# ConvNeXt-V2 block: the order of SyncE's DMA issues within a slot

## Chip, cores and metric

The kernel runs on one core of a Trainium2 chip. The metric is the device time of one execution in microseconds (us). SyncE (SP) computes nothing here; it issues DMAs from one list, in the order of the program, and where an issue has to wait, all that stands behind it waits too.

## What is computed

One block on an image of 512 x 512 pixels with 96 channels, in bf16: a depthwise 3x3 convolution, a layer norm over the channels, a product with w1 (96 to 384), GELU, a global response norm over all pixels, a product with w2 (384 to 96), and the residual.

```
out = sum over i, j of xp[:, i:i+H, j:j+W, :] * dw[i, j]
h = layernorm(out)
h = gelu(h @ w1)
gx = sqrt((h * h).sum(axis=(1, 2)) + 1e-6)
nx = gx / (gx.mean(axis=-1) + 1e-6)
h = grn_gamma * (h * nx) + grn_beta + h
return x + h @ w2
```

The response norm needs the sum of squares of h over the whole image, so the kernel makes two passes.

## The kernel before

The image is cut into 128 blocks of 4 rows. The **first pass** makes conv, layer norm, the w1 product, GELU and the sums of squares. The **second pass** (lines 1017 to 1040) makes or reloads h for each block, multiplies by w2 and adds x. The change lies in the first pass alone.

The first pass is a software pipeline over slots (the loop at line 838), one block per slot in the steady part. A block goes through these stages, each in a later slot than the one before. Each engine's instructions are kept in program order (the class InOrder, so most lines of the profile read L35, its helper).

- `load_x(s + 4)`: SP loads block s + 4 into `xin` (4 buffers). `turn_x(s + 3)`: DVE transposes block s + 3 into `xT`; a block loaded in slot s is thus turned in slot s + 1, in the middle of DVE's work there.
- `conv_taps(s)`: PE makes the convolution, and ACT, in some slots helped by DVE, copies it out of PSUM to `y_bf` (`evac`).
- `stage_sq`: POOL squares `y_bf` (`ysq`). `stage_stats`: PE sums y and y squared over the channels. `stage_moments`: DVE scales the sums.
- For each batch of four blocks: `stage_rstd` and `stage_newton`, twelve small POOL operations that make the reciprocal standard deviation (`var`, `ri`, `nt`, `rn`, `rstd`); `stage_turn`, a DVE transpose to `rt` in the same slot as the Newton steps; one slot later `stage_rows`, two SP DMAs that write `rt` to `r_dram`; one slot later `stage_bcast`, four SP DMAs that read it back to all partitions as `rbc` (3 buffers).
- `stage_norm`: POOL multiplies `y_bf` by `rbc` to `yn` (3 buffers). The first norm of a batch comes one slot after the broadcast.
- One slot later `stage_write`, four SP DMAs of `yn` to `yn_dram`; one slot later `stage_read`, one SP DMA back to `ynT` in the layout that PE needs; two slots later the w1 product of that block (`mlp_units`), GELU on ACT into `g`, `bn_stats` on DVE (`bst`) for the sums of squares, and Gram products on PE for the rest.
- `store_next`: SP writes a third of a finished `g` to `g_dram`, for blocks whose h is kept for the second pass.

The table built at lines 798 to 832 says in which slot each stage of each block or batch falls. Rows and broadcast of one batch thus never fall into the same slot; of four slots one has rows and the next one the broadcast. Within a slot the order of SP's issues is the order of the calls at lines 840 to 850. POOL's order in a slot is newton, square, norm, rstd. The first four blocks and the last fourteen go other ways: the first make their rstd on DVE and PE, without rows and broadcast, and after the conv of block 127 the slots have the w1 product alone (`mlp_tail`).

Of the kernel before, what the change touches and what calls it, by code (L numbers as in the profile page):

```python
# [56 lines left out]
def kernel(  # L57
# [129 lines left out]
    with ExitStack() as p1:  # L187
# [31 lines left out]
        def load_x(b):  # L219
            t = xinpool.tile([128, SL, C], bf16, name="xin")  # L220
            off = x.offset + b * GR * W * C
            rows = lambda p0, p1, s0, s1: (
                t[p0:p1, s0:s1, :].rearrange("p g c -> p (g c)"),
                bass.AP(x.tensor, off + (p0 * PXP - 1 + s0) * C, [[PXP * C, p1 - p0], [1, (s1 - s0) * C]]))
            if b == 0:
                pool.memset(t[0:1, 0, :], 0.0)
                parts = [(16, 128, 0, SL), (0, 16, 1, SL), (1, 16, 0, 1)]
            elif b == NBLK - 1:
                pool.memset(t[96:128, SL - 1, :], 0.0)
                parts = [(0, 112, 0, SL), (112, 128, 0, SL - 1), (112, 127, SL - 1, SL)]  # L230
            else:
                parts = [(0, 128, 0, SL)]
            for part in parts:
                o, i_ = rows(*part)
                sp.dma_start(out=o, in_=i_)
            xins[b] = t
# [377 lines left out]
        def stage_rows(k):  # L614
            b0, n = BATCHES[k]
            rt = rts.pop(k)
            N = n * GR * NG
            nq, nt = min(32, N), (N + 31) // 32
            with nc.allow_non_contiguous_dma("small rows of rstd"):
                if nq == 32:  # L620
                    for t in range(nt):
                        sp.dma_start(
                            out=r_dram[b0:b0 + n].rearrange("b r w -> (b r w)").rearrange(
                                "(t q a p) -> t a q p", q=32, a=4, p=32)[t],
                            in_=rt[:, 32 * t:32 * t + 32])
                else:
                    for a in range(4):
                        sp.dma_start(
                            out=r_dram[b0:b0 + n].rearrange("b r (g m) -> (b r g) m", g=NG)[:, 32 * a:32 * a + 32],
                            in_=rt[32 * a:32 * a + nq, :32])  # L630

        def stage_bcast(k):
            b0, n = BATCHES[k]
            rbc = rbcpool.tile([128, BATCH, W], bf16, name="rbc")
            for j in range(GR):
                sp.dma_start(out=rbc[32 * j:32 * j + 32, :n, :].rearrange("p n w -> p (n w)"),
                             in_=bass.AP(r_dram[b0].tensor, r_dram[b0].offset + j * n * W, [[0, 32], [1, n * W]]))
            rbcs[k] = rbc
# [9 lines left out]
        def stage_write(b):  # L648
            yn = yns.pop(b)
            for r in range(GR):  # L650
                sp.dma_start(out=yn_dst(b, r), in_=yn[32 * r:32 * r + 32, :, :])
# [101 lines left out]
        def store_next():  # L753
            if stores:
                b, h = stores.pop(0)
                n = NCH * QW * NQ // 3
                sp.dma_start(out=g_dram[whole.index(b)][:, h * n:h * n + n],
                             in_=flat(b)[:, h * n:h * n + n])
# [78 lines left out]
        turn_x(2)  # L837
        for s in range(last_slot + 1):
            get = lambda kind: at.get((s, kind), [])
            if s + 4 < NBLK:  # L840
                load_x(s + 4)
            for b in get("read"):
                stage_read(b)
            for b in get("write"):
                stage_write(b)
            for k in get("bcast"):
                stage_bcast(k)
            for k in get("rows"):
                stage_rows(k)
            store_next()  # L850
            for k in get("newton"):
                stage_newton(k, pool)
# [218 lines left out]
```

## Time and profile before

| | |
|---|---|
| median of the 3 runs | 1477.81 us (1477.04 to 1479.55) |
| span of the profiled execution, first to last instruction (no other time is listed for it) | 1475.6 us |
| busy share of the span: PE, DVE, ACT, POOL | 94%, 80%, 95%, 88% |
| DMA issues of SP in the change: rows, broadcasts | 62 of 8 KB, 124 of 128 KB |
| other DMA issues of SP in the first pass: x loads, yn writes, yn reads, g stores | 132, 512, 128, 105 |
| length of one norm, one square on POOL | 3.11 us, 2.76 us |

The span can be read in stretches: to about 70 us the start, to 870 the steady first pass, to 973 its end without convolutions, and then the second pass. A wait in the profile is the idle time of an engine ahead of an instruction, with the name of what released it; for a wait on a DMA the name is that of an issue near the release, and it can be that of a neighbour in SP's queue. SP's own lines give the time in which it issued, not the time of the transfer.

### The profile page before, as it was taken

What the parts mean: (1) busy time and instruction counts of PE and PEld (TensorE: products, weight loads), DVE (VectorE), ACT (ScalarE), POOL (GpSimd) and SP (SyncE); (2) the same over time, 40 slices, a digit from 0 to 9 for tenths busy, and PEclk for the clock granted to TensorE, in tenths of its full rate; (3) what the DMA queues carried; (4) which work ended last, traced back from release to release, by engine and by line L of the source; (5) the groups of instructions that cost most, each with busy time, mean ns of one, the idle gap of its engine ahead of it and who ended that gap; (6) DMA issues with size and microseconds to landing.
All of it is one profiled execution on the core that took longest, in us unless ns stands there. A gap on an engine that the chain in (4) does not pass through costs nothing.

```text
span 1475.6 us, 54538 instructions
## 1 busy us (share of the span) xinstructions
PE 1394.1 (94%) x23125; PEld 810.0 (55%) x23125; DVE 1183.4 (80%) x2174; ACT 1405.9 (95%) x1595; POOL 1300.9 (88%) x923
## 2 busy tenths in 40 slices
PE   8889899999899999999999998889999999999998
PEld 3434444444444444444444445457777777777776
DVE  8849989999899999999999997965555555555555
ACT  7889999999899999999998999999999999999997
POOL 3469989998899999999999998379999999999998
PEclk9999999999999999999999999999999999999999
DMA  6677778888788888888898876669999999999998
GB/s 180 197 204 231 245 231 275 249 266 240 244 254 268 262 275 239 271 258 272 249 276 247 267 230 200 177 226 366 358 328 383 402 392 392 405 381 406 389 390 315
DMA packets 167913, 422.03 MB, mean 286 GB/s; under 512 B 34326, under 2 KB 84182, under 8 KB 163190
## 3 DMA queue, kind: packets, MB, share of 16 engines
q1 hardware_dynamic: 151428, 314.98, 66.0%
q0 software_dynamic: 14880, 103.43, 18.6%
q8 instruction: 181, 2.97, 0.8%
q14 instruction: 62, 0.51, 0.1%
q10 hardware_dynamic: 1362, 0.15, 0.1%
HBM read 262.16 MB, written 156.22 MB: 284 GB/s over the span
## 4 chain that ended last, share of the span: by engine, by line
POOL 31%; PE 22%; ACT 13%; DVE 12%; DMA 11%; issue 7%; SPq 3%; POOLq 0%; ACTq 0%; DVEq 0%
PE PS L35 22%; POOL xb L328 17%; ACT g L35 8%; DVE bst L35 8%; POOL yn L35 7%; DMA xin<-in_x_dram 3%; ACT y_bf L35 3%; SPq L35 3%; DMA ynT<-yn_dram 3%; POOL xr L283 2%; DMA rbc<-r_dram 2%; DVE xT L35 2%; DMA yn_dram<-yn 2%; POOL ysq L35 1%; POOL var L35 1%
## 5 line engine op out<-in xcount | busy, mean ns | idle before, releaser
L35 ACT ACTIVATE g<-PS 128x512 bf16<-128x512 f32 (+2 forms) x1062 | 730.7, 842 | 26.0 <-PE PS L35 22.4
L35 DVE BATCH_NORM_STATS2 bst<-g 128x6 f32<-128x512 bf16 x1110 | 673.0, 672 | 23.5 <-ACT g L35 23.4
L35 ACT ACTIVATE gr<-PS 128x1536 bf16<-128x1536 f32 x360 | 498.5, 1457 | 14.8 <-PE PS L35 10.0
L35 POOL TENSOR_TENSOR yn<-y_bf,rbc 128x1536 bf16<-128x1536 bf16 x126 | 391.6, 3111 | 84.1 <-DMA rbc<-r_dram 50.5
L35 DVE TENSOR_TENSOR o_sb<-PS,xb 128x384 bf16<-128x384 f32 x512 | 277.7, 556 | 221.3 <-PE PS L35 172.0
L35 PE MATMUL PS<-xT,Wq 64*32 64x511 bf16 (+1 forms) x9198 | 347.6, 388 | 29.2 <-DVE y_bf L35 11.7
L328 POOL TENSOR_TENSOR xb<-xr,B2c 128x1536 f32<-128x1536 bf16 x118 | 368.4, 3136 | 1.5
L35 PE MATMUL PS<-ynT,w1p 128*128 128x512 bf16 x1161 | 332.7, 383 | 24.0 <-ACT g L35 5.8
L35 POOL TENSOR_TENSOR ysq<-y_bf 128x1536 bf16<-128x1536 bf16 x114 | 314.1, 2756 | 11.0 <-ACT y_bf L35 9.6
L35 PE MATMUL PS<-ynT,w1s 128*128 128x512 bf16 x1020 | 275.5, 379 | 0.0
L35 PEld LDWEIGHTS <-gr 128*128 128x128 bf16 x4296 | 212.1, 98 | 61.0 <-issue 3.0
L35 PE MATMUL PS<-W2s,gr 128*128 128x96 bf16 x4224 | 223.4, 206 | 2.0 <-DVE o_sb L35 1.8
L35 PEld LDWEIGHTS <-Wq 64*32 64x32 bf16 x9216 | 111.4, 90 | 201.4 <-issue 159.0
L35 ACT ACTIVATE y_bf<-PS 128x1536 bf16<-128x1536 f32 (+2 forms) x135 | 181.7, 1351 | 15.7 <-PE PS L35 10.6
L35 DVE STREAM_TRANSPOSE xT<-xin 128x576 f32<-128x576 f32 (+1 forms) x256 | 181.4, 748 | 12.8 <-DMA xin<-in_x_dram 10.6
L35 PEld LDWEIGHTS <-w1p 128*128 128x128 bf16 x1161 | 89.8, 98 | 180.3 <-issue 123.3
L35 PEld LDWEIGHTS <-g 128*128 128x128 bf16 (+1 forms) x1707 | 105.5, 98 | 89.1 <-issue 57.0
L35 PE MATMUL PS<-w1p,ynT 128*128 128x256 bf16 (+2 forms) x822 | 125.0, 272 | 8.0 <-ACT xT L35 3.2
L35 PE MATMUL PS<-g 128*128 128x128 bf16 x1464 | 123.1, 221 | 4.1 <-DVE PS L35 4.1
L35 PEld LDWEIGHTS <-w1s 128*128 128x128 bf16 x1020 | 81.9, 98 | 40.5
L35 PEld LDWEIGHTS <-gl 128*128 128x128 bf16 x1680 | 83.1, 98 | 30.0 <-issue 8.9
L35 PE MATMUL PS<-W2s,gl 128*128 128x96 bf16 x1680 | 90.3, 206 | 5.2 <-DVE o_sb L35 4.6
(109 smaller groups left out, 708.4 us busy)
## 6 DMA issues: line engine op xcount, KB each, us to landing
xin<-in_x_dram SPq DMA_DIRECT2D x126, 432.0 KB
g_dram<-g SPq DMA_DIRECT2D x105, 512.0 KB
gl<-g_dram POOLq DMA_DIRECT2D x35, 1536.0 KB, 10.7
yn_dram<-yn SPq DMA_DIRECT2D x512, 96.0 KB
ynT<-yn_dram SPq DMA_DIRECT2D x128, 384.0 KB
out_dram<-o_sb SPq DMA_DIRECT2D x127, 384.0 KB
xr<-in_x_dram POOLq DMA_DIRECT2D x123, 384.0 KB, 6.6
ynT<-yn_dram SPq DMA_DIRECT2D x255, 128.0 KB
```

Of the source, the lines that this page charges most:

```text
L35: r = f(*a, **k)
L283: pq.dma_start(out=xr[:], in_=x[0, r0:r0 + GR].rearrange("r w c -> (r w) c").rearrange("(p g) c -> p g c", g=PXP))
L328: pq.tensor_tensor(out=xb[:], in0=grp[q]["xr"][:], in1=bias[:, None, :].to_broadcast([128, PXP, C]), op=ALU.add)
```

## The change

In each slot SP issues the rows first, then the broadcast, and then the x load, the yn read, the yn writes and the store. Before, rows and broadcast came behind the yn writes. Nothing else changes: the stages stay in their slots, and the other engines keep their order.

```
         for s in range(last_slot + 1):
             get = lambda kind: at.get((s, kind), [])
+            for k in get("rows"):
+                stage_rows(k)
+            for k in get("bcast"):
+                stage_bcast(k)
             if s + 4 < NBLK:
                 load_x(s + 4)
             for b in get("read"):
                 stage_read(b)
             for b in get("write"):
                 stage_write(b)
-            for k in get("bcast"):
-                stage_bcast(k)
-            for k in get("rows"):
-                stage_rows(k)
             store_next()
```

## The prediction

> **What bounds the kernel now.** I read the page first, then the busy times by stretch, the list of waits, the timelines of the engines around the longest stalls, and SyncE's queue. The stretches come first, because an average over the whole span mixes stages with different limits. Each line has the stretch and its length in us, then busy us and instructions of PE, PEld, DVE, ACT and POOL, then granted clock, DMA share and GB/s:
>
> ```profile
> core 0: us, PE busy (x) PEld busy (x) DVE busy (x) ACT busy (x) POOL busy (x), PEclk, DMA share, GB/s
> 270.00:870.00 600.00, 572.95 (x10276) 278.60 (x10278) 586.72 (x1040) 581.94 (x835) 558.20 (x421) 0.99 0.84 257
> 870.00:973.00 103.00, 84.41 (x939) 51.33 (x924) 87.45 (x182) 100.87 (x90) 71.02 (x48) 1.00 0.68 203
> 973.00:1476.00 503.00, 491.88 (x7187) 364.86 (x7185) 278.69 (x518) 481.56 (x349) 473.13 (x280) 1.00 0.97 370
> ```
>
> The first 600 us are the steady part of the first pass. There DVE is busy 97.8% and ACT 97.0%, so DVE is idle only 13.3 us and ACT 18.1 us: whatever a reordering of SyncE's queue can win there lies inside those numbers. From 870 to 973 ACT alone is the limit (100.87 of 103). After 973 the second pass runs, and the change has no instruction in it. Next, who waited for whom in 270 to 870 (us in total, times, longest):
>
> ```profile
> ACT g L35 <- PE PS L35: 14.3, 13, 5.1
> POOL yn L35 <- DMA rbc<-r_dram: 10.7, 9, 2.1
> PE PS L35 <- DVE y_bf L35: 10.3, 10, 4.3
> POOL yn L35 <- DMA xin<-in_x_dram: 9.6, 4, 3.2
> ...
> DVE rt L35 <- POOL rstd L35: 7.7, 5, 2.9
> ```
>
> All of POOL's waits fall on the first normalisation of a batch of four blocks, the one that needs a new rbc. So the four that the view puts down to the x load, and 2.2 us put down to the g store, are waits for rbc too: 22.5 us in 21 batches, 1.1 us each, 3.2 at most. One of them can be followed through four timelines (start, length, instruction, and in brackets the idle time before it):
>
> ```profile
> 368.03 3.11 POOL L35 TENSOR_TENSOR yn<-y_bf,rbc 128x1536 bf16<-128x1536 bf16 x1 [3.23 <-DMA xin<-in_x_dram]
> ...
> 375.69 0.25 DVE L35 STREAM_TRANSPOSE rt<-rstd 128x64 bf16<-128x64 bf16 x1 [2.93 <-POOL rstd L35]
> ...
> 376.56 1.28 PE L35 MATMUL PS<-xT,Wq 64*32 64x512 bf16 x23 [4.30 <-DVE y_bf L35]
> ...
> 378.42 0.60 ACT L35 ACTIVATE g<-PS 128x512 bf16<-128x512 f32 x1 [5.10 <-PE PS L35]
> ```
>
> POOL waits 3.23 us for rbc, so the twelve small operations behind that normalisation, which make rstd, are late. DVE runs in order and has the transpose of rstd at its head: it waits 2.93 us. Behind it stands DVE's copy of a conv result out of PSUM, so PE waits 4.30 us and ACT 5.10. A wait on the least busy of these engines reaches all of them.
>
> **Why rbc is late.** SyncE's queue around one batch, in its present order:
>
> ```profile
> 523.78 2.50 SPq L35 DMA_DIRECT2D yn_dram<-yn  x4
> 526.33 1.17 SPq L35 DMA_DIRECT2D r_dram<-rt  x2
> 527.60 0.41 SPq L35 DMA_DIRECT2D g_dram<-g  x1
> 528.06 0.61 SPq L35 DMA_DIRECT2D xin<-in_x_dram  x1
> 528.85 2.05 SPq L35 DMA_DIRECT2D ynT<-yn_dram  x1
> 530.94 2.56 SPq L35 DMA_DIRECT2D yn_dram<-yn  x4
> 533.54 2.21 SPq L35 DMA_DIRECT2D rbc<-r_dram  x4
> ```
>
> The rows (two DMAs) go out at 526.33 although their source, the transpose, was done at 518.27: they stand behind the yn writes, which wait for a normalisation. The broadcast (four DMAs) goes out at 533.54, behind another x load, read and four writes, and POOL then waits 1.95 us.
>
> **The change, part by part.** Nothing is added or removed: 62 row DMAs and 124 broadcast DMAs move ahead in SyncE's list.
>
> 1. Broadcast. Its place is now right behind the store of the slot before. In the batch shown that is the end of the writes, 526.28, plus 0.41 for the store: 526.75 instead of 533.54, so 6.8 us earlier. Done for every batch from the second on, with the issue times of the timeline and with the yn writes held to the ends of their normalisations, this gives 4.5 to 7.5 us earlier, median 5.4. The longest wait for rbc in the steady part is 3.2 us, so all 22.5 us of POOL's waits should go. Does the broadcast wait for the rows instead? The rows' 64-byte packets end 2.1 us after the first issue; rows at the slot's head leave four to eight us until the broadcast. No.
>
> 2. Rows. At the slot's head they wait for the transpose. Compared with the x load that now opens that slot, the transpose ends up to 2.9 us later in one steady batch (172.81 against 169.89), 1.5 in another, and within 0.8 or earlier in the others. Queued behind it are the slot's x load, yn read, yn writes and store. The writes wait for a normalisation that ends later than that (523.75 in the batch shown) and move by nothing; the read fetches a block that PE uses two slots, some 14 us, later.
>
> 3. x loads. Here the price lies. The slot's first x load now stands behind 1.2 us of row issues and that wait; the load of the broadcast's slot stands behind four broadcasts (2.0 to 3.4 us) but gains the 1.2 us that the rows gave up: net 0.6 to 1.8 us later; the load of the slot after goes some 1.2 us earlier. From the DMA packets of 3,456 bytes, which only x loads have, I took each landing and the time until DVE's transpose of that block: median slack 5.4 us in the rows' slot (least 2.2), 3.4 in the broadcast's slot (least 2.0), 2.5 in the one after (least 0.4). So the slot with least slack gets more, and the two that pay can mostly afford it. Value: 1 us of new DVE waits in all; ends 0 and 21 (1 us a batch).
>
> 4. Steady part, the sum. DVE's waits for rstd (7.7) and for x (2.2, the loads behind the present broadcasts) should go: 9.9 of its 13.3 idle us. As DVE is the busiest, I count 9 of them as time, less 1 from point 3: **8 us**. Ends: 0, if DVE finds other waits, and 13.3, all its idle time.
>
> 5. Start, 70 to 170. POOL's second long wait (7.78 us at 103.17) shrinks by the 4.8 us that rbc comes earlier. Against it, the first rows wait for their transpose until 67.81, and the x load issued at 61.85 moves behind them to 69.1; it had 5.17 us of slack, so DVE waits about 2 us, and the loads issued at 69.60 and 84.78 are 2.5 and 3.0 us later. DVE is busy only 78.5 of these 100 us, ACT 92.2. I take 0, between 3 lost and 2 won.
>
> 6. End, 870 to 973. Two more waits for rbc, 4.42 and 7.18 us, should shrink; but ACT is busy throughout, so this is worth 0. Its cover is ACT itself; were ACT idle, both waits would count. Second pass: 0.
>
> Sum: the profiled span 1475.6 less 8 is 1467.6. The median of the runs shown, 1477.81, is 2.2 us above the span; with that, **1470 us**.
>
> **A rule weighed.** The granted clock fell to 0.50 three times: 3.4 us from 185.7, 3.4 from 376.85, 6.8 from 803.5, each right after a PE gap (1.84, 4.30, 2.43 us). The Trainium skill, "TensorE: Matmul & The Clock Gate" (Part 1), has a gate with a free-running window of 3,413 ns that halves the clock after an idle window; the lengths agree, yet here gaps of half a window were enough. By its penalty, half the throttled time, ending the last two would give 5.1 us more (an estimate from that page and the trace's 10.2 us) and a sum of 13. By the rows DVE was busy 3.40 of 3.40 and 6.77 of 6.80 us in them, so PE's slowness lay beside DVE's work. I stay at 8.
>
> **Rivals.**
> - *The x loads become the wait.* The 512 KB of a broadcast now go into the queue ahead of an x load; at 257 GB/s they take 2.0 us. The median load of that slot would land 0.9 + 2.0 later and keep 0.5 us, so half of them make DVE, the bound, wait. It decides from about 0.5 us per batch, where it eats the gain. At 0.7 us in 21 batches, 14.7 less 9 is 6 slower: 1484. For it: six x waits exist already. Against: loads right behind a broadcast today land 5.4 us after issue, those elsewhere 5.2 to 5.3 (4.5 in the rows' slot). The Trainium skill, "DMA: Bandwidth & Descriptors" (Queues, rings and completion order), says each DMA engine takes descriptors in ring order; by it this delay is real, by these latencies it is hardly seen. Chance 0.18.
> - *POOL catches up but DVE and ACT were full anyway*: idle time comes back elsewhere, 2 us won: 1476. For it: in 470 to 570 DVE is busy 99.5%. Or the rows' wait at the head holds SyncE, and rbc gains little; the times in point 2 speak against that. Chance 0.17.
> - *More comes free*: all 13.3 us of DVE's idle time and 2 us at the start: 1475.6 less 15, with the 2.2: 1463. Chance 0.13.
> - *Forecast*, 4 to 12 us won: 0.52.
>
> **How the numbers follow.** A difference under 0.2%, 3 us, is about what a measurement of this kernel cannot tell from none. Faster: 0.52 + 0.13 = 0.65; same 0.17; slower 0.18. The range reaches from the third rival's 1463 to 1482, short of the slower case's centre, which leaves out some 2 in 10.
>
> **What would show it.** Right: the broadcast's issues follow the store; POOL's waits for rbc in the steady part fall from 22.5 us to a few; DVE's waits for rstd from 7.7 to under 2; the 0.50 clock after a PE gap near 377 is gone; the rstd of two batches end 28.2 us apart instead of 28.7 (171.16 to 888.23 over 25 intervals). Wrong: DVE's transposes of x wait over 10 us for x loads, or POOL's waits go and the interval stays.

## The result, and the profile after

The changed kernel took **1470.08 us** (median of 13 runs, 1463.74 to 1475.70), the kernel before 1477.81 (13 runs, 1471.34 to 1481.83); the ratio is 0.995, interval 0.9935 to 0.9966. Faster by half a per cent, as forecast, and the forecast was 1470. But the parts of the sum are not those that were forecast: the steady part won more, and the end of the first pass gave 6 us back, by something that no step had named.

The profiled execution took 1470.01 us, its span is 1468.2. The stretches again, in the columns of the prediction's first view:

```profile
270.00:870.00 600.00, 581.94 (x10491) 284.14 (x10492) 596.11 (x1058) 593.89 (x855) 568.81 (x433) 1.00 0.86 262
...
966.00:1468.00 502.00, 492.15 (x7186) 365.12 (x7183) 277.69 (x513) 481.42 (x348) 472.79 (x280) 1.00 0.97 369
```

DVE was idle 13.3 us in these 600 and is now idle 3.9; ACT went from 18.1 to 6.1. The second pass is as long as it was, 502. The waits in 270 to 870:

```profile
ACT g L35 <- PE PS L35: 3.4, 9, 0.5
PE PS L35 <- DVE y_bf L35: 1.8, 6, 0.4
```

They were 14.3 and 10.3. The lines of POOL for rbc (10.7), of DVE for rstd (7.7) and of DVE for x (2.2) are gone from this view altogether. SyncE's queue around one batch:

```profile
509.18 1.18 SPq L35 DMA_DIRECT2D r_dram<-rt  x2
...
511.50 3.76 SPq L35 DMA_DIRECT2D yn_dram<-yn  x4
515.37 0.54 SPq L35 DMA_DIRECT2D g_dram<-g  x1
515.95 2.19 SPq L35 DMA_DIRECT2D rbc<-r_dram  x4
518.18 0.42 SPq L35 DMA_DIRECT2D xin<-in_x_dram  x1
```

The rows go out right after their transpose (DVE, to 509.15), the broadcast right after the store, and POOL starts the first norm of that batch at 524.81 with no wait. The places that were followed through four engines in the prediction now read:

```profile
356.36 3.12 POOL L35 TENSOR_TENSOR yn<-y_bf,rbc 128x1536 bf16<-128x1536 bf16 x1
...
368.04 0.23 DVE L35 STREAM_TRANSPOSE rt<-rstd 128x64 bf16<-128x64 bf16 x1
```

No brackets: rstd of this batch was ready at 363.98, 4 us before DVE came to it.

**Where the time went.** ACT's instructions come in the same order in every kernel of this study, so the start of the same instruction can be compared. I cut the first pass at those that in the kernel before start at 60, 270, 870, 950 and 973.4 us (the last is in the first block of the second pass) and read off the us between them, in each profile (the start, 60.4 to 64.2 us long, is left out):

| kernel | 60 to 270 | steady, to 870 | to 950 | to 973.4 | rest | median of runs |
|---|---|---|---|---|---|---|
| before | 210.2 | 599.8 | 80.5 | 22.5 | 502.2 | 1477.81 |
| changed | 208.3 | 587.0 | 81.8 | 28.6 | 502.1 | 1470.08 |
| changed, second profile | 210.8 | 587.0 | 80.6 | 29.1 | 502.9 | 1473.85 |
| e1 broadcast alone | 208.5 | 587.0 | 81.8 | 22.1 | 501.8 | 1464.21 |
| e1, second profile | 206.0 | 586.9 | 80.6 | 22.9 | 502.4 | 1464.03 |
| e2 rows alone | 212.3 | 588.1 | 84.0 | 22.9 | 502.4 | 1474.03 |
| e3 changed, moments later | 209.0 | 586.9 | 81.8 | 22.1 | 501.8 | 1466.16 |
| e4 before, moments later | 209.9 | 595.7 | 81.8 | 26.7 | 503.0 | 1480.40 |
| e6 e3, x load last | 216.3 | 595.9 | 81.7 | 22.1 | 501.9 | 1481.14 |
| e7 e1, moments later | 209.3 | 587.9 | 80.6 | 25.7 | 502.7 | 1467.76 |
| e8 broadcast with the rows | 207.3 | 600.1 | 80.6 | 25.6 | 503.1 | 1485.24 |
| e9 changed, moments on POOL | 209.5 | 587.0 | 80.6 | 22.1 | 501.9 | 1466.04 |
| e10 e1, moments on POOL | 206.2 | 586.9 | 81.8 | 22.1 | 501.9 | 1463.42 |

The median of the kernel before was 1477.3 beside e1 to e4, 1475.5 beside e6 to e8 and 1475.7 beside e9, e10 and the second runs; the ratios below are to these.

The change won 12.8 us in the steady part and 1.8 ahead of it, and lost 7.3 behind it, 6.0 of them in the last stretch of the first pass. Run e4, whose steady part has the instructions and the order of the kernel before, needed 595.7 there, so one profile of that order is good to some 4 us; against e4 the win is 8.7. The changed order is steadier: 586.9 to 587.0 in every profile in which rbc and the x loads are both in time.

The length of the steady part follows DVE's waits for rstd and for x in it. They are 0 in the seven profiles at 586.9 to 587.0. They are 0.6 us in e7 (587.9), 0.9 in e2 (588.1), 6.7 in e4 (595.7), 7.3 in e6 (595.9), 9.9 before (599.8) and 10.7 in e8 (600.1). Each us of these waits thus goes with 1.2 to 1.5 us of time; why it is more than 1 is not shown.

The 1.3 us lost from 870 to 950 are not the change's: its second profile does not lose them. The granted clock is 0.50 for 3.4 us in that stretch in the five profiles that need 81.7 or 81.8 with rbc in time (in the changed kernel from 876.13), and not in the six that need 80.5 or 80.6. Only e2 and e4, where DVE waits 7.6 and 6.6 us for rstd there (3.3 before), stand apart.

**What happens in the last stretch.** DVE makes five small operations on the sums of squares there (`second_moments`), and POOL makes its first three residual additions (`xb`). In the kernel before (POOL and DVE by time):

```profile
955.40 0.24 DVE L35 TENSOR_TENSOR parts<-mom 128x72 f32<-128x72 f32 x1
955.68 0.55 DVE L35 TENSOR_TENSOR parts<-parts,mom 128x72 f32<-128x72 f32 x2
...
958.68 9.27 POOL L35 TENSOR_TENSOR xb<-xr,B2bc_f 128x1536 f32<-128x1536 bf16 x3 [15.28 <-DMA xr<-in_x_dram]
```

and in the changed kernel:

```profile
940.53 9.33 POOL L35 TENSOR_TENSOR xb<-xr,B2bc_f 128x1536 f32<-128x1536 bf16 x3 [16.77 <-DVE bst L35]
...
941.99 1.79 DVE L35 TENSOR_TENSOR parts<-mom 128x72 f32<-128x72 f32 x1
943.81 6.17 DVE L35 TENSOR_TENSOR parts<-parts,mom 128x72 f32<-128x72 f32 x2
```

The same three DVE operations take 7.96 us instead of 0.79. Each ends 0.11 to 0.12 us after one of POOL's additions does (943.77 after 943.66, 946.88 after 946.76, 949.98 after 949.86): they stand still until it is over. POOL and SyncE reach this place 18 us earlier than before, DVE only 13, so the additions now begin ahead of DVE's operations. The Trainium skill, "SBUF — State Buffer" (Who interferes with whom), says that a DVE instruction with two SBUF inputs contends with a GpSimd (POOL) instruction that reads SBUF, that the shared ports are an exclusive lock, and that the order of issue decides who is blocked. These rows agree: the additions, which began first, keep their 3.12 to 3.14 us. Behind those operations DVE owes ACT and PE the last sums, and the second pass can't start without them: PE waits 6.21 us for DVE, until 964.12. Of the 6.0 us lost, 0.8 lie behind that wait: in it, at 961.46, the granted clock falls to 0.50, and from DVE's result to the ACT instruction that ends the stretch it takes 2.03 us, with PE's work between them, instead of 1.19.

### The profile page after: what moved, and what is told of

Read it like the earlier page. It is cut to its first block, busy times and chain, and to the rows that moved or that the text cites. A ratio compares the mean times of both kernels' runs of the same rounds, so it can differ in the third digit from the quotient of the medians.

```text
span 1468.2 us, 54503 instructions
## 1 busy us (share of the span) xinstructions
PE 1392.9 (95%) x23125; PEld 811.3 (55%) x23125; DVE 1187.7 (81%) x2174; ACT 1404.5 (96%) x1595; POOL 1300.0 (89%) x923
## 4 chain that ended last, share of the span: by engine, by line
DVE 36%; PE 28%; POOL 14%; ACT 13%; issue 4%; DMA 2%; SPq 2%; ACTq 0%; POOLq 0%; DVEq 0%
PE PS L35 28%; DVE bst L35 25%; POOL xb L328 11%; ACT g L35 9%; DVE xT L35 7%; ACT y_bf L35 3%; SPq L35 2%; POOL xr L283 1%; DVE y_bf L35 1%; DMA yn_dram<-yn 1%; POOL yn L35 1%; DVE o_sb L35 1%; DMA ynT<-yn_dram 1%; ACT xT L35 1%; DVE parts L35 1%
## 5 line engine op out<-in xcount | busy, mean ns | idle before, releaser
L35 PE MATMUL PS<-ynT,w1p 128*128 128x512 bf16 x1161 | 332.5, 383 | 22.9 <-ACT g L35 5.4
L35 DVE STREAM_TRANSPOSE xT<-xin 128x576 f32<-128x576 f32 (+1 forms) x256 | 181.6, 749 | 14.7 <-DMA xin<-in_x_dram 14.7
```

Of the source, the lines that this page charges most:

```text
L35: r = f(*a, **k)
```

## The experiments

My theory after the result: the change wins what the prediction said, because rbc comes in time, and loses 6 to 7 us at the end because POOL's additions hold up DVE's moments. Rivals: the rows' place wins it; the order of the x loads wins it; the late end has another cause.

**e1, the broadcast alone.** The rows stay behind the yn writes.

```
+            for k in get("bcast"):
+                stage_bcast(k)
             if s + 4 < NBLK:
...
-            for k in get("bcast"):
-                stage_bcast(k)
             for k in get("rows"):
```

> Only the broadcast moves to the head of its slot; the rows stay behind the yn writes. Theory (POOL's wait for rbc is what cost the time, the broadcast's place decides it): the broadcast goes out some 4 to 5 us earlier, POOL's waits in 270 to 870 us fall from 22.5 us to under 4, two batches of rstd lie about 28.2 us apart, and the steady part is about as much shorter as in the changed kernel (12 to 15 us at ACT's instructions around 870 us); whole time 1468 to 1473. Rival (the gain comes from the rows' place, or from both together): half of it or less, 1474 to 1478.

Measured: 1464.21 us (ratio 0.9922, 0.9901 to 0.9942), better than both. The steady part is 587.0, with no wait of POOL for rbc: the broadcast's place is enough. What e1 has over the changed kernel lies in the last stretch, 6.5 us shorter:

```profile
942.13 0.25 DVE L35 TENSOR_TENSOR parts<-mom 128x72 f32<-128x72 f32 x1
942.42 0.55 DVE L35 TENSOR_TENSOR parts<-parts,mom 128x72 f32<-128x72 f32 x2
...
944.46 9.28 POOL L35 TENSOR_TENSOR xb<-xr,B2bc_f 128x1536 f32<-128x1536 bf16 x3 [16.42 <-DMA xr<-in_x_dram]
```

Here the additions begin 1.0 us after the last of DVE's five moment operations (943.46), 4 us later than in the changed kernel, and none of the five is held up.

**e2, the rows alone**, the broadcast in its old place.

> Only the rows move to the head of their slot; the broadcast stays behind the yn writes. Theory: rbc arrives at most 1.2 us earlier, most of POOL's 22.5 us of waits stays, and so does the time: 1475 to 1480. Rival (the rows' place is what counts): 1468 to 1472.

Measured: 1474.03 (0.9984, 0.9972 to 0.9996), just faster and 1 us under the expectation. The sum hides a miss of the theory. The steady part is 588.1, nearly as short as with everything moved, although POOL still waits 13.6 us for rbc, the two lines of its first normalisations taken together (12.4 and 1.2):

```profile
POOL yn L35 <- DMA rbc<-r_dram: 12.4, 12, 1.7
...
DVE rt L35 <- POOL rstd L35: 0.9, 1, 0.9
```

So it is not the sum of POOL's waits that cost time. With the rows out of the way rbc and the next x loads come 1.2 us earlier, POOL's longest wait is 1.7 us instead of 3.2, and DVE's wait for rstd falls from 7.7 to 0.9. POOL's lateness costs time only where it is long enough to make DVE stand. Of e2's win in the steady part 2.1 us are lost from 60 to 270, where DVE waits 12.5 us for x loads (8.5 before), and 3.5 from 870 to 950, where it waits 7.6 for rstd (3.3 before).

**e3, the changed kernel with the moments one slot later.**

```
-                second_moments(0, NACC - 1)
             if s == last_slot - 1:
+                second_moments(0, NACC - 1)
```

> The changed kernel with DVE's five operations on the first 25 groups of moments moved one slot later, behind the block that POOL's three residual additions now overlap. Theory (in the changed kernel these DVE operations, 1.79 and twice 3.07 us instead of 0.25 each, are held up by POOL's additions, which read SBUF at the same time, and give back some 7 us of the gain): all five take 0.2 to 0.3 us, the first pass ends 5 to 7 us earlier than in the changed kernel, 1463 to 1465. Rival (the late end of the first pass has another cause, such as ACT's pace or the half clock there): 1469 to 1471.

Measured: 1466.16 (0.9925, 0.9908 to 0.9941); the operations took 0.21 to 0.26 us each and the last stretch 22.1 instead of 28.6. The time is 1 us above the range expected.

**e4, the same move in the kernel before.**

> The kernel before with the same move of DVE's five operations and nothing else. Theory (there POOL's additions began after them, so nothing was held up): no change, 1475 to 1480. Rival (the move helps by itself): 1470 to 1473.

Measured: 1480.40 (1.002, 1.0003 to 1.0037), slower: a small miss, for no change was expected. The profile says why: in this kernel the move puts the operations into the additions instead of out of them.

```profile
955.90 9.30 POOL L35 TENSOR_TENSOR xb<-xr,B2bc_f 128x1536 f32<-128x1536 bf16 x3 [15.91 <-PE PS L35]
...
960.70 1.52 DVE L35 TENSOR_TENSOR parts<-mom 128x72 f32<-128x72 f32 x1
962.25 3.35 DVE L35 TENSOR_TENSOR parts<-parts,mom 128x72 f32<-128x72 f32 x2
```

Its last stretch is 26.7, 4.2 longer than before. The loss follows the overlap, not the move and not the order of SyncE's queue.

**e7, e1 with the moments one slot later.**

> Run e1 (broadcast alone first) with DVE's five moment operations one slot later, as in run e3. Theory: in run e1 those operations ended only 1.2 us before POOL's additions, so they were not held up in its profile; the move makes that certain: 1463 to 1465, none of the runs near 1470. Against run e3 it shows what the rows' place costs: if the rows at the head cost time at the start of the pass by holding back x loads, this one is 1 to 3 us faster than e3; if not, the same.

Measured: 1467.76 (0.995, 0.9931 to 0.9969): a miss; by its ratio it stands with the changed kernel's first runs and not with e1, though the intervals overlap. In e1 the additions come late, and the move carried DVE's operations right into them:

```profile
945.79 9.30 POOL L35 TENSOR_TENSOR xb<-xr,B2bc_f 128x1536 f32<-128x1536 bf16 x3 [16.93 <-DMA xr<-in_x_dram]
...
952.14 3.36 DVE L35 TENSOR_TENSOR parts<-parts,mom 128x72 f32<-128x72 f32 x2
```

So the run says nothing of what the rows' place costs. A place in time is no cure for such a meeting; the next change of pace brings it back.

**e9 and e10, the moments on POOL**, in the changed kernel and in e1: POOL then makes them ahead of its additions, in its own order.

```
-        def second_moments(k0, k1):
+        def second_moments(k0, k1, eng=dve):
...
-            dve.tensor_tensor(out=p, in0=v[:, :, :, :, 1], in1=v[:, :, :, :, 1], op=ALU.mult)
+            eng.tensor_tensor(out=p, in0=v[:, :, :, :, 1], in1=v[:, :, :, :, 1], op=ALU.mult)
...
-                second_moments(0, NACC - 1)
+                second_moments(0, NACC - 1, pool)
```

> The changed kernel with the first group's five moment operations on POOL instead of DVE, in their old place: POOL makes them ahead of its residual additions, so the two can't meet on two engines. Theory (DVE's operations with two SBUF inputs stand still while POOL's additions run): the loss of 7 us at the end of the first pass is gone whatever the timing, 1463 to 1466, and the additions begin some 3 us later. Rival (DVE was slow for another reason, or POOL's five operations are as costly): 1468 or more.

> Broadcast alone first (run e1) with the five moment operations on POOL as in run e9. Theory: no collision, as in the profile of run e1, 1462 to 1466. Against e9 it shows what the rows' place costs or brings: rows at the head hold back x loads at the start, so this one is up to 2 us faster.

Measured: e9 1466.04 (0.9928, 0.9900 to 0.9957), e10 **1463.42** (0.9913, 0.9883 to 0.9943), the lowest median of all. e9 is at the upper end of its range, and its additions begin 4.9 us later than in the changed kernel, where 3 were expected. In e9:

```profile
943.47 0.31 POOL L35 TENSOR_TENSOR parts<-mom 128x72 f32<-128x72 f32 x1 [17.29 <-DVE mom L35]
943.86 0.79 POOL L35 TENSOR_TENSOR parts<-parts,mom 128x72 f32<-128x72 f32 x2
...
945.47 9.27 POOL L35 TENSOR_TENSOR xb<-xr,B2bc_f 128x1536 f32<-128x1536 bf16 x3
```

On POOL they cost 1.7 us of a stretch in which it waits anyway, and the last stretch is 22.1 in both. Over the runs this stretch follows the time that DVE's five operations lose to the additions: nothing lost in e3 and e6, 22.1 us; 3.0 and 2.9 us lost in e7 and e8, 25.7 and 25.6; 4.1 in e4, 26.7; 7.2 and 7.7 in the changed kernel, 28.6 and 29.1.

What the rows' place costs would be seen from 60 to 270: with rows first 208.3, 210.8, 209.0 and 209.5 (changed twice, e3, e9), with rows last 208.5, 206.0, 209.3 and 206.2 (e1 twice, e7, e10), 1.9 us apart in the mean but overlapping. The intervals of e9 and e10 overlap too. And the clock was at 0.50 for 3.4, 13.7, 10.2 and 10.2 us there in the first four and for 6.8, 0, 6.8 and 0 in the others, so a cost of the rows' place is not shown.

**The changed kernel and e1 once more, on one chip.**

> The changed kernel once more, on the same chip as the other three: 1468 to 1472, with the moment operations held up by POOL's additions as in its first profile.

> Run e1 once more, on the same chip as the changed kernel: if the 6 us between them are the collision alone, its profile has the five moment operations clear of POOL's additions and the time is 1463 to 1467; if its moment operations collide in this profile, the time is near the changed kernel's.

Measured: the changed kernel 1473.85 (0.9976, 0.9954 to 0.9998), above the range expected; e1 1464.03 (0.9917, 0.9885 to 0.9948). In the changed kernel's second profile the three operations take 8.5 us beside the additions, in e1's again 0.8. Of the 5.9 us between the medians of the first runs, and the 9.5 between these two profiles, the last stretch shows 6.5 and 6.2: that much goes with the meeting. In the second pair 2.8 us more lie ahead of 270, with the clock at 0.50 for 13.7 us from 60 to 270 in the changed kernel and never in e1. The runs of the changed kernel spread from 1464.6 to 1480.1 here, those of e1 from 1462.6 to 1467.5; only two of the former were profiled, so that the meeting is what spreads them is argued, not shown.

**e6, e3 with each x load behind the yn writes**, which charges the rival's price.

> The kernel of run e3 with each slot's x load moved behind the yn writes, next to the store: rows, broadcast, read, writes, x load, store. It charges the rival's price on purpose: every x load leaves some 3 to 5 us later, where the measured slack of the loads is 3 to 6 us at the median. Theory: the waits of DVE's x transposes in 270 to 870 us stay under 10 us in all, and the time is within 4 us of run e3 (1466 to 1470). Rival (x loads are the tight transfer): tens of us of such waits, 1475 or more.

Measured: 1481.14 (1.0039, 1.0019 to 1.0058), slower than before: my expectation was wrong by 11 us. POOL hardly waits for rbc, but in 270 to 870:

```profile
PE PS L35 <- DVE y_bf L35: 7.8, 10, 1.9
...
DVE xT L35 <- DMA xin<-in_x_dram: 7.3, 10, 2.0
```

The median time from an x load's landing to its transpose is 0.7 to 2.0 us here against 3.4 to 5.9 in the changed kernel, and DVE stands, and PE behind it. The waits of the x transposes stay under the 10 us expected; what they cost was underrated. The steady part is 9.0 us longer than e3's for these 7.3 us of DVE's waits, and from 60 to 270 it loses 7.3 more.

**e8, the broadcast one slot earlier**, right behind the rows, everything else in the old order, the moments later.

```
-                put(last_s + 4, "bcast", k)
+                put(last_s + 3, "bcast", k)
...
-            for k in get("bcast"):
-                stage_bcast(k)
             for k in get("rows"):
                 stage_rows(k)
+            for k in get("bcast"):
+                stage_bcast(k)
             store_next()
```

> No x load stands behind a row or a broadcast of its own slot: the old order of the slot, but the broadcast goes out one slot earlier, right behind the rows, with DVE's moments one slot later as in run e3. SyncE waits about 1 us for the rows to land. Theory (what counts is that rbc is there in time, whichever way): POOL's waits for rbc in 270 to 870 us under 4 us, 1463 to 1467. Rival (the gain comes from the order of x loads against rows and broadcast): 1472 to 1478.

Measured: 1485.24 (1.0069, 1.0042 to 1.0097), the slowest of all, and the theory as I had put it falls: rbc is in time (POOL's first normalisations wait 3.6 us in the steady part, 1.3 at most) and nothing is won.

```profile
DVE xT L35 <- DMA xin<-in_x_dram: 10.7, 9, 2.9
```

The x load of the next slot now follows the rows, the wait for them, the broadcast and the g store within 4.2 us. In the batch at 436 us it is issued at 438.61 and its first packet starts 2.2 us later, 1.2 in the same batch of e7, where the store goes out ahead of the broadcast; the median time from landing to transpose is 1.0 us in that slot, 3.4 in e7. The larger part of this is the place in SyncE's list: in the median the load is issued 6.7 us ahead of its transpose, 8.2 in e7. The rest is the transfer: it lands 5.6 us after the issue, 4.9 in e7. The Trainium skill, "DMA: Bandwidth & Descriptors" (Queues, rings and completion order), which the prediction weighed, says that each DMA engine takes descriptors in ring order. This run agrees: with 1 MB of broadcast and store ahead of it, the x load lands 0.7 us later after its issue than in e7.

## Why the prediction was right, point by point

1. *Broadcast*: right. It follows the store, and all of POOL's 22.5 us of waits in the steady part are gone (one of 1.0 is left in the second profile).
2. *Rows*: right. They wait for their transpose in most batches, and nothing behind them is late in the steady part.
3. *x loads*: right in the steady part, where the value was 1 us of DVE waits and none came. e6 and e8 show that the rival was real: with some 2 to 4 us less slack for most of the loads, DVE's waits cost the steady part 9 to 13 us. The change spends less slack than there is. The loads of the rows' slot are issued 1 us closer to their transposes (8.9 us ahead in the median, 9.9 before) and land 1 us faster; those of the broadcast's slot kept a median slack of 3.4 us, as before, and those behind them went from 2.5 to 5.9.
4. *Steady part*: the mechanism is right, DVE's waits for rstd and x being what POOL's lateness costs; the size was 8, and 12.8 was measured between the two first profiles, 8.7 against e4. I had counted 9.9 us of DVE's waits as 9, less 1 for new ones; no new ones came, and by the runs each us of such waits is worth 1.2 to 1.5. The cause has to be put more narrowly than I did: e2 shows that POOL may go on waiting, up to 1.7 us at a batch, for nothing.
5. *Start*: 0 was expected between 3 lost and 2 won; 1.8 were won in the first profile and 0.6 lost in the second. DVE's waits for x from 60 to 170 grew from 8.5 to 14.7 us in the first profile, more than the 2 us named, and yet the stretch was not longer.
6. *End*: **this step failed.** Its words were that two more waits for rbc would shrink and that this was worth 0, because ACT is busy throughout. They shrank (4.42 to 0.71, 7.18 to 4.99) and won nothing; but POOL's earlier additions met DVE's moments and cost 6.0 us in the last stretch. I had asked what covers a gain, and not what an engine that gets ahead would start earlier, and beside whom. The 8 us of step 4 were too few and the 0 of this step too favourable. The two errors nearly cancelled, so that the sum came out at 1470 is in part luck.

*The clock.* The half clock near 377 is gone, as one of the signs asked for. But e4's profile, with the old order, has none there either, so that sign proves nothing; that the change removes it is not shown. Nor does the half clock set the steady part: e4 has none in it, the kernel before 10.2 us, and both fit DVE's waits alike (6.7 us and 8.7 above 587.0; 9.9 and 12.8). So, as far as these profiles show, it was right not to add the 5 us of the rule weighed. One reading there was loose: at 803.51 the clock fell inside PE's gap, which ended at 804.40, and not behind it.

*Interval of rstd*: 28.16 us over the same 25 intervals, 28.2 expected.

## What to carry to other kernels

In a list of DMA issues, put a small transfer that an engine waits for ahead of what stands waiting itself, but count the slack of each load that it passes: here 1 us was free, and 2 to 4 us cost more than the whole win. When a change lets an engine that is off the path run ahead, look at what it will then do earlier and at who works beside it; a cure is to give both pieces of work to one engine's own order, not to move one of them in time. A total that comes out as forecast says nothing of its terms: compare the start of the same instruction at several places.

## What I had not expected of the hardware

DVE operations of 0.25 us with two operands in SBUF took up to 3.07 us beside POOL additions of 3.1 us, one addition for one operation, in four kernels (changed, e4, e7, e8). DVE's bn_stats, with one operand, ran beside POOL all along: 0.672 us in the mean before and 0.673 after. In the kernel before, a piece of this had been there unseen: one of the same operations at the very end of the pass took 2.02 us instead of 0.17 and ended at 967.98, POOL's addition at 967.95. The same operation is held up in e1 (1.05 us, 2.16 in its second profile), e2 (2.50), e9 (0.69) and e10 (1.09), so e9 and e10 take away only the larger part of the meeting.
